# Two layers of attention and MLP on one core: which score maxima are taken beside the projections, the pace there, and attention's written-out order

## The chip, the cores and the metric

The kernel runs on 1 core of one Trainium2 chip. The metric is the device time of one execution in microseconds (us). The engines are PE (matmuls; its weight loads are listed as PEld), DVE, ACT, POOL, and SP, which only issues DMAs here.

## The reference, cut to what matters

x has 2048 rows of 640; there are 32 heads of 20. The same two blocks run twice, with the same weights. All is fp32.

```
def _A_ref(x, wqkv, wo):
    qkv = (x @ wqkv).reshape(B, S, 3, H, Dh).transpose(2, 0, 3, 1, 4)
    q, k, v = qkv[0], qkv[1], qkv[2]
    scores = einsum("bhqd,bhkd->bhqk", q, k) * (Dh ** -0.5)
    p = softmax(scores, axis=-1)
    o = einsum("bhqk,bhkd->bhqd", p, v)
    return o.transpose(0, 2, 1, 3).reshape(B, S, D) @ wo
def _B_ref(x, w1, b1, w2, b2):
    h = x @ w1 + b1
    return (where(h > 0, h, 0) ** 2) @ w2 + b2

for _ in range(2):
    x = x + _A_ref(layernorm(x), wqkv, wo)
    x = x + _B_ref(layernorm(x), w1, b1, w2, b2)
```

The softmax is over 2048 keys, so each query of each head needs the maximum over its 2048 scores before its exponentials are taken.

## The kernel before, in words

**Precision and packing.** Operands are split into a high and a low part (F32R), and products are the sum of three partial ones. A head's scores take 60 partitions: query parts and key parts stacked. Two heads stand on partitions 0 to 59 and 64 to 123 of one tile, and their matmuls are issued one after the other on the two halves of PE. Four heads (two such pairs) are a group: eight groups, g = 0 to 7. Queries come in four blocks of 512 (qb), keys in four chunks of 512 (c). A block of attention is one (g, qb), numbered t = 4 g + qb, 32 in all; it has 16 key tiles of 128.

**A layer's stages.** `qkv` (projections, and maxima beside them), `attention`, then the output projection and the MLP. All engines' instructions stand in the order in which the Python code emits them; nothing is scheduled afterwards.

**Maxima.** They are computed by score matmuls with queries on the partitions (L654), in steps of (p, sub): p picks a pair of heads, sub a quarter of the query block; eight steps are a (g, qb, c). Two ways:
- *plain*: `smax` and `smax_two` reduce one chunk's scores on DVE (L665 in attention, L679 in `qkv`).
- *double*: two chunks at once. max(a, b) = a + relu(b - a). `d_kd` holds the difference of the keys of chunks 1 and 0 ("d") and 3 and 2 ("e"). `step_two` multiplies queries by the differences, and ACT takes the Relu (L687); `both_two` multiplies by the lower chunk's keys, and one DVE instruction (L694) adds both and keeps the maximum, followed by one that reads its accumulator. A double step is two matmuls of differences, two of keys, two Relus, two pairs of DVE instructions.

**Projections.** `qkv` goes through UNITS, numbered n: a unit is one of ten 128-row pieces (pos; ORDER maps it to keys or queries, and jj is the piece) for one of four blocks of 512 tokens (tb). The first FIRST = 4 pieces come token block by token block (n = 0 to 15), the others piece by piece. From n = 4 on each matmul is cut in two halves of 64 partitions, the second halves lagging 22 behind (`Halves`, L356 and L365). After each chain's first half a 1x1 DVE copy (`turned_t`, L358) reads its bank. After the 40 units come 16 v units of 320 columns (`v_unit`, tt), and then the lagging halves are caught up. `between(cost)` is called after each matmul; costs are 1 for q/k and 0.65 for v. When the sum of costs reaches the pace, `some()` emits one piece of maxima work: a plain pair (pace PLAIN_PACE) or one half of a double step, `step_two` or `both_two` (pace DOUBLE_PACE). STEPS says at which n a group of maxima or a list of DOUBLE joins the queue. What is left when all units are emitted is emitted in a loop after them, ahead of attention. These matmuls write PSUM banks 0 to 4 in turn (`ps_q`), the projections banks 5 to 7.

`proj_end` evicts a unit: it splits it into high and low parts on ACT and POOL. For key pieces 0 and 1 (`which and pos < FIRST`), it also keeps the even token block in `kf`, subtracts it from the odd one on POOL, splits the difference, and stores it to `d_kd`. `load_kd` loads differences (six DMAs), `load_k` keys (six DMAs), `load_q` queries. Piece jj holds rows 128 jj to 128 jj + 127; group g needs rows 80 g to 80 g + 79. `following` calls `tiles` for a group of maxima when it begins and for the next two after it. DOUBLE and the plain groups of before cover all maxima of groups 0, 1 and 2 (t = 0 to 11).

**Attention.** `attention` emits by the letters of a written-out order; ORDER_OF_BLOCK is repeated until all is done:
- a, b: scores of one head (L748) and its exponential (L758, 512 wide), for the first or second half of PE
- S: both heads at once, into two adjacent banks, with one exponential over 1024
- m, n: one maximum (`smax`, L654 and L665), first or second half
- V: values of one key tile for four heads (L763), which wait for that tile's exponentials, accumulated in bank 7

Banks 0 to 6 are given out by `Clock`, a table of expected times. The maxima of later blocks (`todo`) are taken ahead of their use; when `todo` is empty, m and n emit nothing. After a block, DVE copies the accumulator (L776) before the next block's first values may write it. `load_q` for a block and key loads for later groups are emitted in `begin`.

Of the kernel before, what the change touches and what calls it, by code (L numbers as in the profile page):

```python
# [9 lines left out]
F32R = mybir.dt.float32r  # L10
# [6 lines left out]
P = 128  # L17
# [7 lines left out]
QB = 512  # L25
NQB = S // QB
# [7 lines left out]
NBLK = NG * NQB  # L34
# [5 lines left out]
def tile_layers(  # L40
# [11 lines left out]
    nc = tc.nc  # L52
# [6 lines left out]
    dram = ctx.enter_context(tc.tile_pool(name="dram", bufs=1, space=DRAM))  # L59
# [3 lines left out]
    def name(p):  # L63
        n_alloc[0] += 1
        return f"{p}{n_alloc[0]}"

    def slot(shape, dtype, label):
        return arena.tile(shape, dtype, tag="slot", name=name(label))

    def dma(eng, dst, src):  # L70

        if dst.dtype == F32R:
            dst = dst.bitcast(F32)
        if src.dtype == F32R:
            src = src.bitcast(F32)
        eng.dma_start(dst, src)  # L76

    def xtile(label):
        return xpool.tile([P, D], F32, tag="x", name=name(label))
# [146 lines left out]
            sp.put(raw, k * 4, k * 4 + 2, 2, eng_hi, eng_lo)  # L226

    d_qk = dram.tile([2, 2, D, S], F32R, name="d_qk")
    d_kd = dram.tile([2, 2, 2 * P, QB], F32R, name="d_kd")
    d_v = dram.tile([S, H, 32], F32, name="d_v")  # L230
    d_o = dram.tile([D, NQB, 2 * QB], F32R, name="d_o")
    d_one = dram.tile([2, 2, QB], F32R, name="d_one")
# [21 lines left out]
    def split_to(dst_hi, dst_lo, src):  # L254

        nc.scalar.copy(dst_hi, src)
        nc.vector.tensor_sub(dst_lo, src, dst_hi.bitcast(F32))  # L257

    def split_on_pool(dst_hi, dst_lo, src, r=None, hi=None):

        if r is None:
            r = xtile("r")[:, :QB]
        nc.scalar.copy(r, src)
        (hi or pool_hi)(dst_hi, r)
        pool_lo(dst_lo, r, dst_hi.bitcast(F32))

    def pool_hi(dst, src):
        nc.gpsimd.tensor_copy(dst, src)  # L268

    def pool_lo(dst, a, b):  # L270
        nc.gpsimd.tensor_sub(dst, a, b)
# [68 lines left out]
    xt_, keys = {}, {}  # L340
# [42 lines left out]
    def proj_end(pos, tb, dst):  # L383
        ev = slot([P, 2, QB], F32R, "ev")
        which, jj = divmod(ORDER[pos], 5)
        rows = slice(jj * P, (jj + 1) * P)
        kd = None
        if which and pos < FIRST:


            if tb % 2 == 0 and jj == 0:
                keys["of"] = slot([P, 2, QB], F32, "kf")
            kf = keys["of"][:, jj, :]
            r = xtile("r")[:, :QB] if tb % 2 else kf
            split_on_pool(ev[:, 0, :], ev[:, 1, :], dst, r, nc.scalar.copy)
            if tb % 2:
                kd = slot([P, 2, QB], F32R, "kd")
                nc.gpsimd.tensor_sub(kf, r, kf)
                pool_hi(kd[:, 0, :], kf)
                pool_lo(kd[:, 1, :], kf, kd[:, 0, :].bitcast(F32))  # L400
                if jj:
                    del keys["of"]
        else:
            if tb or pos >= FIRST:
                split_on_pool(
                    ev[:, 0, :], ev[:, 1, :], dst, None, nc.scalar.copy if pos < FIRST else None
                )
            else:
                split_to(ev[:, 0, :], ev[:, 1, :], dst)

        def store():
            cols = slice(tb * QB, (tb + 1) * QB)
            dma(nc.sync, d_qk[which, :, rows, cols].rearrange("h p t -> p h t"), ev)
            if kd is not None:
                dma(nc.sync, d_kd[tb // 2, :, rows].rearrange("h p t -> p h t"), kd)

        return store
# [105 lines left out]
    k_t, q_t, v_t, mx_t, kept = {}, {}, {}, {}, {}  # L523
# [79 lines left out]
    def rows_of_heads(dst, src_of, segs, g):  # L603
        for par in range(2):
            for off, hl in segs:
                r0 = 64 * par + off
                src = src_of[hl, 4 * g * DH : (4 * g + 4) * DH]
                src = src.rearrange("(a b d) t -> b d a t", a=2, b=2)[par]
                dma(nc.sync, dst[r0 : r0 + DH], src)

    def load_k(g, c, keep):

        if not keep:
            k = slot([P, 2, QB], F32R, "k")
        elif (g % 4, c) in kept:
            k = kept[g % 4, c]
        else:
            k = kept[g % 4, c] = slot([P, 2, QB], F32R, "k")
            for par in range(2):
                dma(nc.sync, k[64 * par + 60 : 64 * par + 62], d_one)  # L620
        k_t[g, c] = k
        rows_of_heads(k, d_qk[1, :, :, c * QB : (c + 1) * QB], KSEG, g)

    def load_q(t):
        g, qb = divmod(t, NQB)
        q_t[t] = slot([P, 2, QB], F32R, "q")
        rows_of_heads(q_t[t], d_qk[0, :, :, qb * QB : (qb + 1) * QB], QSEG, g)
# [16 lines left out]
    def maxima(t):  # L644
        if t not in mx_t:
            mx_t[t] = small.tile([P, 4, 4, 4], F32, tag="mx", bufs=14, name=name("mx"))
            if t in PARTLY:
                nc.vector.memset(mx_t[t], LEAST)
# [182 lines left out]
    def prep_job():  # L831
# [15 lines left out]
    DOUBLE = [  # L847
        [],
# [5 lines left out]
    ]  # L854
    PARTLY = {g * NQB + qb for x in DOUBLE for g, qb, c in x}

    FIRST = 4
    PLAIN_PACE = 4.2  # L860
    DOUBLE_PACE = 1.97
    STEPS = {
        2: [("tiles", (0, 0, 0))],
        4: [("plain", (0, 0, 0)), ("tiles", (1, 0, 0))],
# [5 lines left out]
        12: [("double", 1)],  # L870
        15: [("double", 2)],
        19: [("double", 3)],
    }
    UNITS = [(tb, pos) for tb in range(NQB) for pos in range(FIRST)]
    UNITS += [(tb, pos) for pos in range(FIRST, 10) for tb in range(NQB)]

    def qkv(first, x_src, rest):

        pending, groups, work = [], [], []
        double, twos, begun = [], [], []  # L880
# [34 lines left out]
        def later(f, n):  # L915
            pending.append((state["n"] + n, f))
# [16 lines left out]
        def end_group(x):  # L933
            g, qb, c = x
            t = g * NQB + qb
            rest = [w[0] for w in work[:1] + twos[:1]] + [w[0][0] for w in begun[:1]] + groups + double
            if t == 0:
                left[t] -= 1 if c in range(4) else 2
                if left[t] == 0:
                    mrows_max(t)  # L940
                    store = mrows(t)
                    later_rows.append((state["n"] + 60, store))
                    later_rows.append((state["n"] + 75, lambda: mrows_load(t)))
            if (t or left[t]) and all(y[:2] != (g, qb) for y in rest[:4]):
                del q_t[t]
            use = {(y[0], y[2]) for y in rest + coming}
            use |= {(h, 2 * "de".index(y)) for h, y in use if y not in range(4)}
            for y in [y for y in k_t if y[0] == g and y not in use]:
                if g < 2 or y[1] not in range(4):
                    del k_t[y]  # L950
# [22 lines left out]
        def some():  # L973
# [4 lines left out]
            if begun and (len(begun) > 1 or not (double or twos)):  # L978
# [6 lines left out]
                if (p, sub) == PAIRS[-1]:  # L985
                    end_group(w[0])
                return DOUBLE_PACE
            if groups or work:
# [3 lines left out]
            if w:  # L992
                (g, qb, x), p, sub = w
                begun.append((w, step_two(g * NQB + qb, p, sub, x)))
            return DOUBLE_PACE

# [34 lines left out]
        for tt in range(NKT):  # L1031

            def end(store, tt=tt):
                later(store, 12)
                if tt % 4 == 3:
                    del xt_[tt // 4]

            v_unit(tt, run, end)
            if first:
                w_v.save_full(1)  # L1040
            if tt == 10:
                load_v(0, 0)
            if tt in (8, 9):
                for c in (0, 1) if tt == 8 else (2, 3):
                    assert (0, c) not in k_t
                    load_k(0, c, True)
            if tt == 11:
                load_k(3, 0, True)
                load_q(3 * NQB)
            if tt == 12:  # L1050
                for c in range(1, 4):
                    load_k(3, c, True)
            if tt == 13:
                load_q(1)
                load_q(3 * NQB + 1)
        while run.behind:
            run.catch()
        while double or twos or begun:
# [11 lines left out]


    ORDER_OF_BLOCK = (
        "bbannaVbamnabmVnabmnabVSnanbmVnambabmVSbmnaVSnabmVSnSmVbmamnSVbmanbanVan"
        "abmbmVbambannVbmabanmVSmbanVSnabmVSnSmVm"
    )

    def attention(first, x_src, first_rows):
        last = NBLK * NKT
# [3 lines left out]
        st_n, sm_n = [0, 0], [0, 0]  # L1082
        state = {"begun": -1, "done": 0, "acc": None, "debt": 0}
        clock = Clock()
        todo = [
            (t, p, sub, c)
            for t in range(NBLK)
            for c in range(4)
            for p, sub in PAIRS
            if (t, p, sub, c) not in done  # L1090
        ]
# [104 lines left out]
        for o in "abab":  # L1196
            op(o)
        while state["done"] < last:
            for o in ORDER_OF_BLOCK:
                op(o)  # L1200
        assert min(sm_n) == len(todo)
        q_t.clear()
# [227 lines left out]
```

## Time and profile before

| | us |
|---|---|
| median of 3 runs (3583.65 to 3587.55) | 3584.02 |
| the profiled execution, its own time | 3588.35 |
| its span | 3586.5 |
| layer 1, projections: start to the first values of attention | 343.87 |
| layer 1, attention: first to last values | 343.87 to 1387.2 |
| layer 2, first values of attention | 2124.62 |

| engine | busy us | share |
|---|---|---|
| PE | 3557.8 | 99% |
| DVE | 2650.9 | 74% |
| ACT | 2694.0 | 75% |
| POOL | 836.0 | 23% |

How to read what follows: a window's row has its limits and length, then for each engine the busy time and, in brackets, the number of instructions, then the granted share of the TensorE clock, the DMA engines' share and GB/s. With a filter only the filtered instructions are counted. A row of the order of time has start, duration, engine, line, operation, tiles written and read, and the count of merged instructions; in square brackets stands how long the engine was idle before and what ended the wait. A group's row has the count, the busy time and the mean duration in ns, then idle time before it. Matmuls are pipelined, so their durations overlap: the distance between starts is what a matmul costs.

### The profile page before, as it was taken

Reading aid. Unit: us, or ns where it says so; the run is one execution under the profiler, and the core shown is the slowest. Engines: PE = TensorE matmul, PEld = TensorE weight load, DVE = VectorE, ACT = ScalarE, POOL = GpSimd, SP = SyncE. Lnnn points to the kernel's source line nnn. Section 1 sums busy time; section 2 is a strip of 40 time slices with the busy share of each in tenths; the row PEclk is TensorE's granted clock in tenths of the full one; section 3 lists DMA queues with packets and bytes.
Section 4 is the critical chain, followed back from the end, with each engine's and each line's share of the span. In section 5 each row is a group of like instructions: output and inputs, shape, how many; then the busy total and the mean of one; then the engine's idle time right before and its main releaser. Section 6 shows DMA issues by size and latency. Waiting matters only on the chain.

```text
span 3586.5 us, 71057 instructions
## 1 busy us (share of the span) xinstructions
PE 3557.8 (99%) x25544; PEld 2151.0 (60%) x25544; DVE 2650.9 (74%) x5208; ACT 2694.0 (75%) x4742; POOL 836.0 (23%) x945
## 2 busy tenths in 40 slices
PE   8999999999999999999999999999999999999999
PEld 7998333333333336889989973333333333378998
DVE  8998888888888871445569988888888888625443
ACT  3888999999999994122238889999999999932221
POOL 5440334312121210122143201212112212101110
PEclk9999999999999999999999999999999999999999
DMA  7766454422212136622367552222222121365220
GB/s 242 231 223 198 138 170 147 141 78 71 60 49 60 54 102 218 234 74 74 103 193 226 191 174 67 79 73 63 67 83 56 42 60 51 111 234 209 75 81 37
DMA packets 282800, 433.85 MB, mean 121 GB/s; under 512 B 71188, under 2 KB 130324, under 8 KB 282448
## 3 DMA queue, kind: packets, MB, share of 16 engines
q1 hardware_dynamic: 281920, 427.61, 38.3%
q8 instruction: 202, 3.31, 0.4%
q10 hardware_dynamic: 528, 1.70, 0.2%
q14 instruction: 150, 1.23, 0.1%
HBM read 284.48 MB, written 144.68 MB: 120 GB/s over the span
## 4 chain that ended last, share of the span: by engine, by line
PE 94%; DMA 2%; DVE 1%; ACT 1%; SPq 0%; issue 0%; POOL 0%; ACTq 0%; DVEq 0%; POOLq 0%
PE banks L763 27%; PE banks L336 22%; PE banks L748 18%; PE banks L654 17%; PE banks L365 5%; PE banks L356 4%; ACT e L758 0%; SPq L76 0%; DMA k<-d_qk 0%; PE banks L461 0%; DMA ot<-d_o 0%; DVE r L1278 0%; DVE h L257 0%; ACT r L1277 0%; DVE mx L679 0%
## 5 line engine op out<-in xcount | busy, mean ns | idle before, releaser
L758 ACT ACTIVATE e<-banks 128x512 f32<-128x512 f32 (+1 forms) x3460 | 2040.8, 687 | 49.4 <-PE banks L748 11.5
L665 DVE TENSOR_REDUCE mx<-banks 128x1 f32<-128x512 f32 x2560 | 1620.7, 685 | 326.1 <-PE banks L654 294.4
L763 PE MATMUL banks<-e,vg 128*32 128x512 f32 x8192 | 1097.3, 605 | 6.1 <-ACT e L758 5.4
L654 PE MATMUL banks<-k,q 60*128 60x512 f32 x3392 | 1080.6, 411 | 6.3 <-DMA q<-d_qk 1.8
L748 PE MATMUL banks<-q,k 62*128 62x512 f32 x4096 | 1045.5, 441 | 0.0
L748 PEld LDWEIGHTS banks<-q,k 62*128 62x128 f32 x4096 | 514.5, 185 | 741.8 <-ACT e L758 467.6
L654 PEld LDWEIGHTS banks<-k,q 60*128 60x128 f32 x3392 | 579.3, 185 | 208.0 <-ACT e L758 64.7
L694 DVE CUSTOM_DVE_ANT_0 rl<-banks,rl 128x512 f32<-128x512 f32 x704 | 456.7, 688 | 24.5 <-PE banks L654 6.2
L687 ACT ACTIVATE rl<-banks 128x512 f32<-128x512 f32 x704 | 381.0, 601 | 52.3 <-PE banks L654 41.8
L763 PEld LDWEIGHTS banks<-e,vg 128*32 128x32 f32 x8192 | 163.8, 108 | 362.3 <-issue 262.6
L336 PE MATMUL banks<-w,h 128*128 128x320 f32 x2304 | 348.9, 310 | 2.6 <-DVE h L257 2.5
L1277 ACT ACTIVATE r<-banks,b_t 128x512 f32<-128x512 f32 x96 | 66.1, 688 | 377.8 <-PE banks L336 224.7
L336 PEld LDWEIGHTS banks<-w,h 128*128 128x128 f32 x2304 | 339.2, 188 | 11.4 <-DVE h L257 6.4
L336 PE MATMUL banks<-xnT,w 128*128 128x512 f32 x1440 | 329.7, 389 | 0.0
L365 PE MATMUL banks<-xnT,wqk 64*128 64x512 f32 x1080 | 327.3, 393 | 1.6 <-DVE turned_t L358 1.6
L356 PE MATMUL banks<-xnT,wqk 64*128 64x512 f32 x1080 | 327.2, 394 | 0.0
L336 PEld LDWEIGHTS banks<-xnT,w 128*128 128x128 f32 x1440 | 269.5, 188 | 55.3
L807 POOL TENSOR_TENSOR few<-few,minus_t 128x16 f32<-128x16 f32 x62 | 179.8, 2900 | 225.6 <-DMA few<-d_s 225.6
L654 PE MATMUL banks<-kd,q 60*128 60x512 f32 x704 | 208.9, 398 | 0.2
L365 PEld LDWEIGHTS banks<-xnT,wqk 64*128 64x128 f32 x1080 | 201.2, 187 | 12.9 <-DVE turned_t L358 2.1
L268 POOL CAST mr<-nt 128x32 fp32r<-128x32 f32 x64 | 13.4, 210 | 824.6 <-DVE nt L720 794.6
L356 PEld LDWEIGHTS banks<-xnT,wqk 64*128 64x128 f32 x1080 | 198.8, 186 | 10.2 <-issue 1.7
(91 smaller groups left out, 2789.5 us busy)
## 6 DMA issues: line engine op xcount, KB each, us to landing
q<-d_qk SPq DMA_DIRECT2D x888, 80.0 KB
d_qk<-ev SPq DMA_DIRECT2D x80, 512.0 KB
k<-d_qk SPq DMA_DIRECT2D x456, 80.0 KB
x<-d_x SPq DMA_DIRECT2D x96, 320.0 KB
d_o<-ot SPq DMA_DIRECT2D x248, 80.0 KB
ot<-d_o SPq DMA_DIRECT2D x38, 512.0 KB
d_v<-v SPq DMA_DIRECT2D x32, 512.0 KB
vg<-d_v SPq DMA_DIRECT2D x32, 512.0 KB
```

Of the source, the lines that this page charges most:

```text
L336: nc.tensor.matmul(dst, a, b, start=(n == 0), stop=(n == last))
L356: nc.tensor.matmul(dst, a[:64], b[:64], start=start, stop=last)
L365: nc.tensor.matmul(dst, a, b, start=False, stop=last, skip_group_check=True)
L654: nc.tensor.matmul(dst, q_t[t][b : b + 60, p, sub * P : (sub + 1) * P], k_t[t // NQB, c][b : b + 60, p, :], start=True, stop=True,)
L665: nc.vector.tensor_reduce(maxima(t)[:, 2 * p + par, sub, c : c + 1], dst, axis=AX.X, op=ALU.max)
L687: nc.scalar.activation(r, dst, AF.Relu)
L694: nc.vector.tensor_tensor_reduce(out=r[par], in0=dst, in1=r[par], scale=1.0, scalar=LEAST, op0=ALU.add, op1=ALU.max, accum_out=maxima(t)[: ...
L748: nc.tensor.matmul(dst, k_t[t // NQB, kt // 4][b : b + 62, p, (kt % 4) * P : (kt % 4 + 1) * P], q_t[t][b : b + 62, p, :], start=True, stop ...
L758: nc.scalar.activation(dst, src, AF.Exp, scale=SCALE)
L763: nc.tensor.matmul(acc[32 * h : 32 * h + 32, :], v_t[t // NQB, kt // 8][:, kt % 8, 32 * h : 32 * h + 32], es[p][:, par, :], start=(kt == 0 ...
L807: nc.gpsimd.tensor_tensor(few, few, minus_t, op=ALU.pow)
L1277: nc.scalar.activation(r, dst, AF.Relu, bias=b1_t[:, f : f + 1])
```

## The change

- A fifth list in DOUBLE: both doubles of group 3, query block 0 (t = 12), 16 steps. It joins the queue at n = 26. Their maxima leave attention's `todo`.
- Differences are now also made for key piece 2 (`jj < 3`), whose high part is cast on POOL as before; `d_kd` has a third piece.
- DOUBLE_PACE goes from 1.97 to 1.84.
- The loads at the end of `qkv` skip keys of group 3 that are already there, and preload queries of t = 13 and 14 (NEXT) in place of 12 and 13.
- ORDER_OF_BLOCK is another string: 20 m and 20 n instead of 21 each, 9 S instead of 10, 23 a and 23 b instead of 22 each, 16 V as before.
- Once `todo` is empty, whole passes of LAST_ORDER (8 S and 4 V) take the place of ORDER_OF_BLOCK.

```
-    d_kd = dram.tile([2, 2, 2 * P, QB], F32R, name="d_kd")
+    d_kd = dram.tile([2, 2, 3 * P, QB], F32R, name="d_kd")
...
-        if which and pos < FIRST:
-            if tb % 2 == 0 and jj == 0:
+        if which and jj < 3:
+            if tb % 2 == 0 and jj != 1:
                 keys["of"] = slot([P, 2, QB], F32, "kf")
-            kf = keys["of"][:, jj, :]
+            kf = keys["of"][:, jj % 2, :]
             r = xtile("r")[:, :QB] if tb % 2 else kf
-            split_on_pool(ev[:, 0, :], ev[:, 1, :], dst, r, nc.scalar.copy)
+            split_on_pool(
+                ev[:, 0, :], ev[:, 1, :], dst, r, nc.scalar.copy if pos < FIRST else None
+            )
...
+        [(3, 0, "d"), (3, 0, "e")],
     ]
+    NEXT = [t for t in range(3 * NQB, NBLK) if (3, t - 3 * NQB, "e") not in DOUBLE[4]]
...
-    DOUBLE_PACE = 1.97
+    DOUBLE_PACE = 1.84
...
         19: [("double", 3)],
+        26: [("double", 4)],
...
-            if tt == 11:
-                load_k(3, 0, True)
-                load_q(3 * NQB)
-            if tt == 12:
-                for c in range(1, 4):
-                    load_k(3, c, True)
+            if tt in (11, 12):
+                for c in (0, 1) if tt == 11 else (2, 3):
+                    if (3, c) not in k_t:
+                        load_k(3, c, True)
+                if tt == 11:
+                    load_q(NEXT[0])
             if tt == 13:
                 load_q(1)
-                load_q(3 * NQB + 1)
+                load_q(NEXT[1])
...
     ORDER_OF_BLOCK = (
-        "bbannaVbamnabmVnabmnabVSnanbmVnambabmVSbmnaVSnabmVSnSmVbmamnSVbmanbanVan"
-        "abmbmVbambannVbmabanmVSmbanVSnabmVSnSmVm"
+        "SnabmVSanmbVSanmbVSSmnVnabbanmVnabanmbVbabmnnaVnaabmbmVbmmbanaVnambmbaVb"
+        "amnmbaVnanbabmVSmnabVSmnabVSnabmVSanmbV"
     )
+    LAST_ORDER = "SSSVSSVSSVSV"
...
-            for o in ORDER_OF_BLOCK:
+            for o in LAST_ORDER if min(sm_n) == len(todo) else ORDER_OF_BLOCK:
                 op(o)
```

## The prediction

> **What bounds the kernel now.** The page first, then windows over the stages, then single instructions in order of time.
>
> ```profile
> span 3586.5 us, 71057 instructions
> PE 94%; DMA 2%; DVE 1%; ACT 1%; SPq 0%; issue 0%; POOL 0%; ACTq 0%; DVEq 0%; POOLq 0%
> ```
>
> The chain that ended last is 94% PE. The change touches two stages of each layer: the projections with the maxima beside them, and attention. How close the other engines follow PE there decides.
>
> First the projections (window, length, busy time and count of an engine; the first two rows are of all engines, then those of L654 on PE, then of L694 on DVE).
>
> ```profile
> 160.00:190.00 30.00, 30.00 (x260) 27.59 (x258) 28.57 (x94) 26.42 (x51) 11.97 (x14) 1.00 0.70 223
> 280.00:310.00 30.00, 30.00 (x360) 29.99 (x358) 29.36 (x99) 26.50 (x54) 1.68 (x4) 1.00 0.69 203
> ...
> 160.00:190.00 30.00, 25.04 (x88) 14.85 (x87) 1.00 0.70 223
> 280.00:310.00 30.00, 24.42 (x89) 15.06 (x89) 1.00 0.69 203
> ...
> 160.00:190.00 30.00, 28.13 (x87) 1.00 0.70 223
> 280.00:310.00 30.00, 28.83 (x89) 1.00 0.69 203
> ```
>
> Matmuls go two by two, one on each half of the partitions; I call two such a row. In the q/k stretch 260 matmuls are 130 rows in 30 us: 0.231 us a row. In the v stretch 89 matmuls of L654 are 44.5 rows, 10.3 us; the other 271 are 135.5 rows of 320 columns in 19.7 us: 0.146 us each. L694 has two instructions for a head, four for a double, so doubles stand 30/(87/4) = 1.379 us apart in the first stretch, 30/(89/4) = 1.348 in the second. By the pace of 1.97, and two calls to a double, 3.94 units lie between doubles: 3.94 q/k rows and two rows of the double are 5.94 x 0.231 = 1.372 us; 3.94/0.65 = 6.06 v rows and two are 0.885 + 0.462 = 1.347. Both are what is seen: PE's rows set the pace, DVE is busy 95 and 98%.
>
> Now the end of the projections, and what DVE can do when it is behind (start, duration, then the instruction).
>
> ```profile
> 336.90 0.69 DVE L694 CUSTOM_DVE_ANT_0 rl<-banks,rl 128x512 f32<-128x512 f32 x1
> ...
> 337.51 0.69 DVE L694 CUSTOM_DVE_ANT_0 rl<-banks,rl 128x512 f32<-128x512 f32 x1
> ...
> 338.12 0.69 DVE L694 CUSTOM_DVE_ANT_0 rl<-banks,rl 128x512 f32<-128x512 f32 x1
> ...
> 338.73 0.14 DVE L358 COPY turned_t<-banks 1x1 f32<-1x1 f32 x1
> 342.94 1.29 DVE L665 TENSOR_REDUCE mx<-banks 128x1 f32<-128x512 f32 x2 [4.07 <-PE banks L654]
> ...
> 338.93 2.02 PE L365 MATMUL banks<-wv,xnT 64*128 64x320 f32 x12 [0.52 <-DVE turned_t L358]
> 340.65 0.50 PE L748 MATMUL banks<-q,k 62*128 62x512 f32 x1
> ...
> 341.23 1.18 PE L748 MATMUL banks<-q,k 62*128 62x512 f32 x5
> ...
> 343.87 0.64 PE L763 MATMUL banks<-e,vg 128*32 128x512 f32 x4
> ```
>
> Back to back a head takes DVE 0.611 us (336.90, 337.51, 338.12), a double 1.222. The last double ends with the last v unit; PE drains its lagging halves, attention's first score starts at 340.65, its first values (L763) at 343.87.
>
> Attention: the starts of the values of successive key tiles, one block of 16 tiles, and the last two blocks.
>
> ```profile
> 366.94 1.07 PE L763 MATMUL banks<-e,vg 128*32 128x512 f32 x8
> ...
> 369.08 1.07 PE L763 MATMUL banks<-e,vg 128*32 128x512 f32 x8
> ...
> 370.98 1.06 PE L763 MATMUL banks<-e,vg 128*32 128x512 f32 x8
> ...
> 374.78 1.06 PE L763 MATMUL banks<-e,vg 128*32 128x512 f32 x8
> ...
> 376.93 1.06 PE L763 MATMUL banks<-e,vg 128*32 128x512 f32 x8
> ...
> 375.92 0.69 DVE L776 COPY o<-banks 128x512 f32<-128x512 f32 x1
> ...
> 376.93:409.62 32.69, 32.69 (x237) 12.65 (x235) 27.52 (x46) 31.93 (x56) 10.73 (x13) 1.00 0.54 166
> 1325.54:1357.33 31.79, 31.14 (x212) 10.27 (x211) 14.17 (x24) 31.23 (x55) 6.50 (x6) 1.00 0.35 104
> 1357.33:1387.20 29.87, 27.47 (x185) 7.60 (x186) 0.00 (x0) 28.70 (x52) 6.07 (x4) 1.00 0.64 204
> ```
>
> A tile of four rows takes 369.08 - 366.94 = 2.14 us, one of three 370.98 - 369.08 = 1.90; the difference, 0.24, is one row again. The old order puts four rows before ten of its 16 values and three before six (counting the longer of the two halves): 10 x 2.14 + 6 x 1.90 = 32.80, measured 32.69. So PE's rows set this stage too, up to block 30, where the maxima run out and ACT takes over:
>
> ```profile
> L758 ACT ACTIVATE e<-banks 128x512 f32<-128x512 f32 x2824 | 1478.2, 608 | 32.3 <-PE banks L748 11.4 <-PE banks L654 1.0
> ...
> L758 ACT ACTIVATE e<-banks 128x1024 f32<-128x1024 f32 x636 | 643.0, 1036 | 17.2 <-PE banks L654 0.2 <-PE banks L748 0.2
> ...
> 1343.49 5.99 ACT L758 ACTIVATE e<-banks 128x512 f32<-128x512 f32 x12
> ```
>
> Twelve narrow exponentials end 5.99 - 0.60 = 5.39 us after the first has ended: 0.490 us each; a wide one takes 1036 - 608 = 428 ns more, 0.918. The old block has 44 narrow and 10 wide: 30.7 us, under PE's 32.7.
>
> **The change part by part**, per layer. Counts are from the built programs' instruction order.
>
> *Maxima moved.* Attention loses 32 pairs (4 chunks x 8 steps), 32 rows; the projections gain 16 doubles of two rows, also 32. PE's matmuls are as many as before, so only packing and place can move the time.
>
> *Blocks of 20 pairs.* The new order has four rows before eight values and three before eight. Over blocks 0 to 29 that turns 60 tiles: 60 x 0.24 = -14.4 us; by the block's own 32.69 against 32.80, I take -14.2. ACT must follow: a three-row tile with a wide exponential is 0.918 + 2 x 0.490 = 1.898 against 1.90, and eight such stand in a row across the block's edge. It just fits (block: 46 narrow and 9 wide, 30.8 against 32.3). The accumulator's copy at the edge ends at 375.92 + 0.69 = 376.61, 1.83 after its values began at 374.78; the next values, now 1.90 after, clear it by 0.07. I cost both at nothing; if that cover goes, ACT's nearest row is four narrow ones, 1.96: up to +0.06 x 240 = +14.4, taken up below as a rival.
>
> *Last tiles in an order of four.* Only block 31 uses it. Both last blocks are ACT's: 31.79 + 29.87 = 61.66, with ACT work of 2 x 30.7. Afterwards 30.8 + 32 x 0.918 = 60.2: -1.3, of which PE's lead in the first eight tiles of block 30 keeps back 0.2: -1.1 (bounds -1.3 and 0).
>
> *Denser doubles.* In the q/k stretch the program has 591 rows where it had 574: 17 x 0.231 = +3.9. In the v stretch 169 rows of doubles for 158: 11 x 0.231 = +2.5. The spacing becomes (3.68 + 2) x 0.231 = 1.312 and 5.66 x 0.146 + 0.462 = 1.288. DVE needs 1.222 and, one per 15 rows, a copy of 0.14: 1.256 and 1.275. That is 96 and 99% of PE's spacing, with five banks between them, so a late DVE stops PE soon. Bounds: nothing, or the old spacing staying, 104 x 0.067 + 84.5 x 0.060 = +12.0. Nearer to the first, since heads do follow each other at 0.611: I take +1.0.
>
> *The tail.* Four doubles are left when the last v unit is done, and stand before attention on PE: six rows. The first score writes bank 0, and the sixth of the eight DVE instructions of these doubles reads that bank. From the first row: 0.5 (a matmul's duration) + 5 x 0.611 + 0.69 = +4.2 where the score stood. Queued behind it: all scores, so ACT's first exponentials and the first values. Bounds: six rows alone, 1.4, and four doubles after a matmul, 0.5 + 4 x 1.222 = 5.4.
>
> *DMAs and POOL.*
>
> ```profile
> L398 POOL TENSOR_TENSOR kf<-r,kf 128x512 f32<-128x512 f32 x8 | 10.6, 1323 | 0.0
> L271 POOL TENSOR_TENSOR kd<-kf,kd 128x512 fp32r<-128x512 f32 x8 | 10.5, 1307 | 0.6
> ...
> L268 POOL CAST kd<-kf 128x512 fp32r<-128x512 f32 x8 | 4.9, 612 | 0.5
> ...
> 1816.81 4.68 DMA k<-d_qk
> ```
>
> 14 more DMAs a layer stand on SP (two stores of key differences, twelve loads of them), and group 3's keys 0 and 2 load earlier. POOL gets three more operations for each of two differences: 1.32 + 1.31 + 0.61 us, in a stretch where it is busy 11.97 of 30. Loads are issued two groups ahead, 16 doubles or 21 us. Hidden, nothing; without that cover a landing like the 4.68 us above, once a layer.
>
> *The clock.* PE's share is low at the stage's end, and in layer 2 the granted clock (third from the end of a window's row) fell there.
>
> ```profile
> 2117.18:2120.59 3.41, 2.88 (x21) 2.61 (x19) 1.68 (x7) 0.42 (x1) 0.00 (x0) 1.00 0.68 267
> 2120.59:2124.01 3.42, 3.42 (x16) 2.96 (x14) 0.00 (x0) 2.07 (x5) 0.00 (x0) 0.50 0.24 99
> 2124.01:2127.42 3.41, 3.41 (x15) 1.20 (x15) 1.63 (x4) 2.39 (x6) 0.47 (x2) 0.50 0.48 148
> ...
> 2118.91 2.19 PE L365 MATMUL banks<-wv,xnT 64*128 64x320 f32 x12 [0.53 <-DVE turned_t L358]
> ...
> 2158.77 1.06 PE L763 MATMUL banks<-e,vg 128*32 128x512 f32 x8
> ```
>
> From the drained halves to the end of block 0 layer 2 takes 2158.77 - 2118.91 = 39.86 us, layer 1 376.93 - 338.93 = 38.00: the half clock cost 1.9. With PE waiting for DVE in the tail, layer 1 will meet it too: +1.9 once (bounds 0 and 3.8).
>
> The Trainium skill, page "TensorE: Matmul & The Clock Gate", section "Part 1: The HAM clock gate", says that the clock halves after an idle window of some 3.4 us and returns after a busy one. The length agrees (two windows of 3.41 at 0.50), the condition does not: the window before held 21 matmuls and waited only 0.53 us. By that condition the tail, with a matmul every 0.6 us or so, would cost nothing here and the forecast would be 3577.
>
> **Sum.** A layer: -14.2 - 1.1 + 3.9 + 2.5 + 1.0 + 4.2 = -3.7; two layers -7.4; the clock +1.9: -5.5 us. Against the profiled execution's 3588.35 that is 3582.9; against the median of the runs, 4.3 lower, 3578.5.
>
> **Rivals.**
> *The tail is hidden.* DVE has caught up, and only the six rows are paid; no stalls, no half clock: 2 x (-14.2 - 1.1 + 3.9 + 2.5 + 1.4) = -15: 3569. For it: DVE sat 4.07 us idle at this place. Against: the bank of the first score.
> *Attention is ACT's.* The eight tiles in a row have 0.002 us to spare. At half of the 0.06 each, +7.2 a layer: -5.5 + 14.4 = +8.9: 3593. Against: three such tiles stand in a row already, at 1.90. This would also be the change not doing what its 20 pairs say.
> *Slower: doubles keep their spacing.* The place is the bank ring between PE and DVE: if a double's round trip and not PE's row count makes 1.379 and 1.348, a smaller pace buys nothing. +12.0 - 1.0 = +11 a layer: -5.5 + 22 = +16.5: 3600. It decides from 2.8 us of stalls a layer beyond the 1.0. Against: the rows account for the spacing to 0.01 us.
>
> **How the numbers follow.** Forecast 0.48 (3574 to 3586), tail hidden 0.26, ACT 0.15, spacing 0.11. The range 3567 to 3593 leaves out the last and the edges. This measurement can tell 0.2%, 7.2 us, from no change. Faster by more: the hidden tail and a fifth of the forecast, 0.35; slower by more: the spacing and half of ACT, 0.18; same 0.47.
>
> **What would show it.** Attention's blocks at 32.2 to 32.3 us with eight tiles at 1.90 (at 1.93 or more, ACT wins). Doubles 1.31 and 1.29 us apart. First values of layer 1 about 11 to 12 us later than 343.87. A half clock in both layers near there. DVE idle ahead of attention gone. I am wrong if blocks stay near 32.7, or doubles at 1.35.

## The result, and the profile after

The changed kernel takes 3596.07 us (median of 8 runs, 3594.09 to 3600.69), the one before 3584.28 in the same comparison (8 runs, 3583.65 to 3587.55): ratio 1.0033, interval 1.0022 to 1.0044. It is slower by 0.33%, more than the 0.2% that this measurement can tell, and lies above the predicted range.

The profiled executions stand 3597.91 to 3588.35, +9.6 us; the medians differ by 11.8, since the profiled execution of the kernel before lies above all eight of its runs. By stages, in us, from starts of instructions in the trace (blocks 30 and 31 to the end of the last values):

| | before, layer 1 / 2 | after, layer 1 / 2 | predicted difference, a layer |
|---|---|---|---|
| first to last projection matmul | 326.4 / 315.6 | 341.6 / 325.3 | +7.4 |
| last projection matmul to first values | 2.8 / 3.2 | 8.6 / 8.1 | +4.2, clock +1.9 once |
| attention, first to last values | 1042.2 / 1043.6 | 1030.3 / 1029.9 | -15.3 |
| of it, block mean (1 to 29) | 32.71 / 32.73 | 32.35 / 32.32 | -0.47 |
| of it, blocks 30 and 31 | 61.61 / 61.54 | 59.56 / 59.54 | -1.1 |

Attention gives 12.0 and 13.7 us, the stages ahead of it take 21.0 and 14.6, the rest differs by -0.3. So the slowdown is in the projections and the tail behind them. Lines of the changed kernel stand two lower: L654, L694, L748, L763 of before are L656, L696, L750, L765. First windows over the projections, all engines:

```profile
130.00:160.00 30.00, 30.00 (x254) 27.37 (x251) 28.95 (x99) 26.82 (x54) 16.37 (x18) 1.00 0.67 222
160.00:190.00 30.00, 30.00 (x257) 29.01 (x255) 29.05 (x96) 26.93 (x52) 11.98 (x14) 1.00 0.73 232
280.00:310.00 30.00, 30.00 (x352) 29.63 (x350) 29.52 (x100) 26.85 (x55) 1.67 (x4) 1.00 0.56 168
1955.00:1985.00 30.00, 30.00 (x255) 28.27 (x253) 29.07 (x97) 26.09 (x51) 11.86 (x14) 1.00 0.60 177
```

The same view for L696 on DVE alone:

```profile
160.00:190.00 30.00, 28.67 (x89) 1.00 0.73 232
280.00:310.00 30.00, 29.05 (x91) 1.00 0.56 168
```

PE issues 254 to 257 matmuls in 30 us of the q/k stretch where it issued 260, and never shows as idle: the ends of matmuls are modelled in this profile, so small delays do not appear, and the count is the measure. Over three windows of each stretch (91, 89, 89 and 93, 91, 93 instructions of L696) doubles stand 1.338 and 1.300 us apart; before it was 1.379 and 1.348, by rows it should be 1.312 and 1.288.

The tail, in order of time: DVE, then PE.

```profile
352.95 0.14 DVE L358 COPY turned_t<-banks 1x1 f32<-1x1 f32 x1
355.99 0.69 DVE L696 CUSTOM_DVE_ANT_0 rl<-banks,rl 128x512 f32<-128x512 f32 x1 [2.90 <-PE banks L365]
...
360.27 0.69 DVE L696 CUSTOM_DVE_ANT_0 rl<-banks,rl 128x512 f32<-128x512 f32 x1
...
352.39 3.09 PE L365 MATMUL banks<-wv,xnT 64*128 64x320 f32 x20
...
356.74 0.50 PE L656 MATMUL banks<-k,q 60*128 60x512 f32 x1 [0.35 <-DVE mx L696]
...
359.80 2.87 PE L750 MATMUL banks<-q,k 62*128 62x512 f32 x7 [0.72 <-DVE mx L696]
```

And the windows of the clock there:

```profile
356.80:360.20 3.40, 2.45 (x8) 0.97 (x8) 3.40 (x11) 1.66 (x4) 0.00 (x0) 1.00 1.02 407
360.20:363.60 3.40, 2.93 (x10) 1.59 (x9) 1.46 (x5) 2.81 (x5) 0.00 (x0) 0.50 0.23 93
363.60:367.05 3.45, 3.45 (x13) 1.16 (x15) 1.03 (x3) 1.54 (x4) 0.46 (x2) 0.50 0.90 200
```

DVE stands idle for 2.90 us while PE drains the lagging halves with no maxima between them; then eight heads follow at 0.611 us, the first score waits for the sixth of them, and the clock halves for 6.8 us, two windows.

Attention: the starts of the values around a block's edge and the copy that frees the accumulator:

```profile
460.49 1.07 PE L765 MATMUL banks<-e,vg 128*32 128x512 f32 x8
462.51 1.06 PE L765 MATMUL banks<-e,vg 128*32 128x512 f32 x8
...
461.68 0.69 DVE L778 COPY o<-banks 128x512 f32<-128x512 f32 x1
```

A window of a block's length, begun two tiles ahead of block 4 (494.81), and the last two blocks:

```profile
490.93:523.22 32.29, 32.28 (x238) 12.27 (x239) 26.42 (x44) 31.53 (x56) 15.50 (x19) 1.00 0.55 170
1335.94:1367.36 31.42, 30.57 (x209) 9.89 (x209) 11.28 (x19) 31.29 (x56) 6.49 (x6) 1.00 0.35 105
1367.36:1395.50 28.14, 27.15 (x184) 7.38 (x183) 0.00 (x0) 27.01 (x30) 6.07 (x4) 1.00 0.59 184
```

The mean over the blocks, tile by tile: 1.977 us at the edge (the tile from 460.49), 1.927 for the fourth, 1.90 for the other six with three rows, 2.12 to 2.14 for the eight with four.

One wait reaches PE in layer 1 that did not before. (In the kernel before, POOL too waits for stores of `ev`, 3.4 us at 146 us in layer 1 and twice in layer 2, but PE does not wait behind it.) The chain of work that ended last, between 205 and 245 us (start, duration, what):

```profile
213.42 4.60 DMA kd<-d_kd
218.04 4.18 DMA k<-d_qk
222.24 0.42 SPq L76
222.75 3.99 DMA d_qk<-ev
```

What SP issued in these microseconds (start, time from the first to the last of a row, count):

```profile
211.29 3.31 SPq L76 DMA_DIRECT2D kd<-d_kd  x6
214.93 3.38 SPq L76 DMA_DIRECT2D k<-d_qk  x6
218.45 3.28 SPq L76 DMA_DIRECT2D q<-d_qk  x6
...
222.75 0.72 SPq L76 DMA_DIRECT2D d_qk<-ev  x1
```

The waits from 222 to 232 us (who waited at which line for whom: total, times, longest):

```profile
POOL ev L268 <- DMA d_qk<-ev: 4.7, 1, 4.7
...
ACT r L263 <- POOL ev L271: 1.9, 1, 1.9
PE banks L656 <- ACT rl L689: 1.6, 1, 1.6
```

The window over this stretch:

```profile
195.00:240.00 45.00, 43.38 (x352) 38.83 (x350) 40.08 (x134) 38.59 (x75) 24.91 (x27) 0.96 0.71 235
```

SP issues one DMA after the other: eighteen loads of differences, keys and queries from 211.29 to 221.73 us, and the store of `ev` only at 222.75. POOL waits 4.7 us for the buffer that this store frees, ACT for POOL, with the Relus queued behind it, and PE 1.6 us for a Relu; one window of half clock follows, 3.4 us from 230.5 (0.96 in the mean over this row).

### The profile page after: what moved, and what is told of

It reads as the page before. It is cut to its first block, busy times and chain, and to the rows that moved or that the text cites. A ratio compares the mean times of both kernels' runs of the same rounds, so it can differ in the third digit from the quotient of the medians.

```text
span 3596.1 us, 71237 instructions
## 1 busy us (share of the span) xinstructions
PE 3564.3 (99%) x25544; PEld 2143.6 (60%) x25544; DVE 2611.4 (73%) x5210; ACT 2711.1 (75%) x4824; POOL 849.4 (24%) x957
## 4 chain that ended last, share of the span: by engine, by line
PE 92%; DMA 2%; ACT 2%; DVE 2%; issue 1%; POOL 1%; SPq 1%; POOLq 0%; ACTq 0%; DVEq 0%
PE banks L765 27%; PE banks L336 21%; PE banks L750 17%; PE banks L656 16%; PE banks L365 5%; PE banks L356 4%; ACT e L760 1%; DMA d_qk<-ev 1%; PE banks L351 1%; SPq L76 1%; DMA kd<-d_kd 1%; PE banks L463 0%; DVE mx L681 0%; DVE r L1284 0%; DVE h L257 0%
## 5 line engine op out<-in xcount | busy, mean ns | idle before, releaser
L667 DVE TENSOR_REDUCE mx<-banks 128x1 f32<-128x512 f32 x2432 | 1548.3, 685 | 369.5 <-PE banks L656 303.3
L765 PE MATMUL banks<-e,vg 128*32 128x512 f32 x8192 | 1094.8, 605 | 4.2 <-ACT e L760 3.0
L750 PE MATMUL banks<-q,k 62*128 62x512 f32 x4096 | 1042.1, 442 | 1.7 <-DVE mx L696 0.7
L656 PE MATMUL banks<-k,q 60*128 60x512 f32 x3328 | 974.1, 410 | 9.3 <-DVE mx L681 3.9
L750 PEld LDWEIGHTS banks<-q,k 62*128 62x128 f32 x4096 | 512.3, 185 | 649.0 <-ACT e L760 396.7
L656 PEld LDWEIGHTS banks<-k,q 60*128 60x128 f32 x3328 | 524.8, 186 | 310.5 <-ACT e L760 201.4
L696 DVE CUSTOM_DVE_ANT_0 rl<-banks,rl 128x512 f32<-128x512 f32 x768 | 492.1, 687 | 28.8 <-PE banks L365 8.1
L689 ACT ACTIVATE rl<-banks 128x512 f32<-128x512 f32 x768 | 415.5, 603 | 52.7 <-PE banks L656 40.9
L765 PEld LDWEIGHTS banks<-e,vg 128*32 128x32 f32 x8192 | 163.7, 108 | 363.1 <-ACT e L760 195.4
L356 PE MATMUL banks<-xnT,wqk 64*128 64x512 f32 x1080 | 337.5, 400 | 0.6 <-ACT r L263 0.6
L365 PE MATMUL banks<-xnT,wqk 64*128 64x512 f32 x1080 | 335.4, 396 | 0.0
L656 PE MATMUL banks<-kd,q 60*128 60x512 f32 x768 | 222.7, 408 | 2.6 <-ACT rl L689 2.4
L356 PEld LDWEIGHTS banks<-xnT,wqk 64*128 64x128 f32 x1080 | 200.3, 190 | 11.8 <-issue 1.7
```

What stands on the lines that cost most here:

```text
L356: nc.tensor.matmul(dst, a[:64], b[:64], start=start, stop=last)
L365: nc.tensor.matmul(dst, a, b, start=False, stop=last, skip_group_check=True)
L656: nc.tensor.matmul(dst, q_t[t][b : b + 60, p, sub * P : (sub + 1) * P], k_t[t // NQB, c][b : b + 60, p, :], start=True, stop=True,)
L667: nc.vector.tensor_reduce(maxima(t)[:, 2 * p + par, sub, c : c + 1], dst, axis=AX.X, op=ALU.max)
L689: nc.scalar.activation(r, dst, AF.Relu)
L696: nc.vector.tensor_tensor_reduce(out=r[par], in0=dst, in1=r[par], scale=1.0, scalar=LEAST, op0=ALU.add, op1=ALU.max, accum_out=maxima(t)[: ...
```

## The experiments

Stage times are those of the table above; layer 1 / layer 2. Where nothing else is said, an edit is to the changed kernel, and ratios are to the kernel before, run beside it on the same chip. Differences from the changed kernel are between comparisons; the medians of the kernel before in these are 3584.28 to 3586.06, so such differences hold to about 2 us.

**The tail: leftover doubles among the lagging halves.**

```
         while run.behind:
             run.catch()
+            if len(run.behind) % 3 == 0 and (double or twos or begun):
+                some()
```

> The four left doubles are emitted among the 22 lagging halves instead of behind them. Theory (in the changed kernel DVE sits idle 2.90 us while PE drains the halves, and then the first score waits for DVE's sixth instruction of the left doubles): the doubles start about 3 us earlier, the first values of attention come 3 to 4 us earlier in each layer, and the half clock after the tail costs less: 3586 to 3590 against 3596. Rival (the tail is PE and DVE work that has to be done somewhere, its order is no matter): the halves end later by what the doubles end earlier, 3594 to 3598.

3587.65 us, ratio 1.0007 [0.9998, 1.0017], 8.4 under the changed kernel. Projections and tail together are 3.5 / 3.0 shorter. The half clock behind the tail is gone in layer 2 (block 0 takes 32.3 us for 34.1) and 3.4 us long instead of 6.8 in layer 1. DVE and PE of this kernel, at the same place:

```profile
353.36 0.67 DVE L696 CUSTOM_DVE_ANT_0 rl<-banks,rl 128x512 f32<-128x512 f32 x1
...
357.77 0.69 DVE L696 CUSTOM_DVE_ANT_0 rl<-banks,rl 128x512 f32<-128x512 f32 x1
...
355.26 0.60 PE L365 MATMUL banks<-wv,xnT 64*128 64x320 f32 x3
357.30 0.50 PE L750 MATMUL banks<-q,k 62*128 62x512 f32 x1
```

The eight heads run from 353.36 on, while the halves drain, and the first score stands at 357.30. Most of the tail's price was the order of emission: of the 5.8 / 4.9 that it had grown by, 2.3 / 1.9 stay with the doubles.

**The buffer: one more slot.** The tiles of the projections come out of an arena of NSLOT slots; the room comes from two small pools.

```
-NSLOT = 42
+NSLOT = 43
-            mx_t[t] = small.tile([P, 4, 4, 4], F32, tag="mx", bufs=14, ...)
+            mx_t[t] = small.tile([P, 4, 4, 4], F32, tag="mx", bufs=13, ...)
-        mr = small.tile([P, 2, 32], F32R, tag="mr", bufs=2, ...)
+        mr = small.tile([P, 2, 32], F32R, tag="mr", bufs=1, ...)
```

> 43 buffers of 4 KB instead of 42 (one buffer of maxima and one of their transposed rows less). Theory (layer 1's stall at 228 us is POOL waiting for a buffer whose store is still queued on SP behind loads of differences; ACT stands behind POOL, Relus behind ACT, PE behind the Relus): the stall and the half clock after it go, layer 1's projections are 3 to 4.5 us shorter, layer 2's within 1 us: 3592 to 3593 against 3596. Rival (SP's queue or the loads themselves are late, and the wait only moves to another instruction): 3595 to 3597, with a PE gap over 1 us elsewhere in layer 1's projections.

3592.09 us, 1.0021 [1.0012, 1.0031], 4.0 under the changed kernel. Its row of the same stretch:

```profile
195.00:240.00 45.00, 45.00 (x384) 40.98 (x381) 42.13 (x141) 40.90 (x80) 25.49 (x27) 1.00 0.72 244
```

32 matmuls more in 45 us, none of which waits visibly, and full clock. The projections are 5.0 / 1.1 shorter. Of the 5.0, 1.6 come ahead of the 1050th projection matmul, before the wait; the buffer is worth the other 3.4. The stretch from the 1050th to the 1140th projection matmul of layer 1 shows it in every kernel: it takes 19.1 us in the changed kernel and 17.9 to 20.1 in the five others below with the dense pace and 42 buffers, 15.7 to 15.8 in the four with 43, and 14.9 to 15.1 in the four with the old pace.

**Both together.**

> Both repairs in one: left doubles among the lagging halves, and 43 buffers. Theory (two separate causes, the tail and layer 1's buffer): they add, 8.4 + 4.0 less than the changed kernel: 3583 to 3585, what the kernel before takes. Rival (both gains were one and the same half clock in layer 1): 3587 to 3588.

3583.51 us, 0.9994 [0.9985, 1.0003]: 12.6 under the changed kernel, the sum of the two within those 2 us. What is left equals the kernel before within the interval.

**The pace alone, in the kernel before** (`DOUBLE_PACE = 1.97` to `1.84`, nothing else).

> The kernel before with DOUBLE_PACE 1.84 alone: the same 22 groups of doubles, done some 45 units earlier. Theory (at the dense spacing DVE is the limit of the stretch, 1.30 to 1.34 us a double where PE's rows would give 1.29 to 1.31): rows that DVE delays are not won back by rows alone at the end, 1 to 3 us a layer: 3586 to 3590; spacing 1.30 in the v stretch. Rival (the dense pace costs nothing by itself, the projections' growth comes from the sixteen further doubles and their differences alone): 3584 within 1.5.

3594.22 us, 1.0025 [1.0016, 1.0034]: +8.6, more than either forecast allowed. The same number of rows takes 332.1 / 317.5 us where it took 326.4 / 315.6, +5.7 / +1.9. 3.1 of the 5.7 lie in the stretch of the late buffer, which the forecast did not have; the rest, 2.6 / 1.9, is within the 1 to 3 us a layer of its theory. Two windows:

```profile
160.00:190.00 30.00, 30.00 (x257) 28.99 (x256) 29.10 (x97) 26.78 (x53) 13.16 (x14) 1.00 0.73 234
1955.00:1985.00 30.00, 30.00 (x254) 28.26 (x253) 29.07 (x97) 26.49 (x52) 11.41 (x14) 1.00 0.54 167
```

And its waits from 205 to 240 us:

```profile
POOL ev L268 <- DMA d_qk<-ev: 5.2, 1, 5.2
...
PE banks L654 <- ACT rl L687: 2.1, 1, 2.1
```

The counts are those of the changed kernel, and the same buffer is late, without the new loads and differences. The denser pace brings both.

**The old pace, in the changed kernel** (`1.84` to `1.97`): (104 + 84.5) x 0.13/1.84 = 13 doubles a layer go from the projections to the tail.

> The changed kernel with the old DOUBLE_PACE of 1.97: some 13 doubles more a layer are left behind the v units. Theory (a double costs two rows, 0.46 us, beside the projections and 1.22 us of DVE in the tail): 13 x 0.76 = +9.9 a layer, less about 2.5 of stalls that the dense pace brings: +7 a layer, 3610. Rival (the dense pace stalls PE as much as it fits in, so that the pace is worth nothing): 3596 within 3 us.

3605.85 us, 1.0059 [1.0044, 1.0074], between the two forecasts. The projections are 16.1 / 13.2 shorter, the tail 18.2 / 18.3 longer. Layer 1's 16.1 holds the 3.4 of the late buffer, which the old pace does not meet. A double beside the projections thus costs (16.1 - 3.4)/13 and 13.2/13, some 1.0 us, where its two rows are 0.46; standing alone, 1.4. A window in the tail of this kernel:

```profile
330.00:360.00 30.00, 29.08 (x159) 20.74 (x156) 25.65 (x83) 22.69 (x44) 0.00 (x0) 0.74 0.66 204
```

**Is DVE the limit at the dense pace?** The 1x1 copy on ACT, on top of both mendings:

```
-                nc.vector.tensor_copy(turned_t, dst[:1, :1])
+                nc.scalar.copy(turned_t, dst[:1, :1])
```

> The kernel with both repairs, and the 1x1 copy after each chain's first half on ACT instead of DVE (some 68 a layer). Theory (at the dense pace DVE, 97 to 98% busy, holds PE's rows back: 254 matmuls in 30 us where there were 260): DVE is freed of 8 to 9 us a layer, the rows return to 258 or more, the projections are 3 to 5 us a layer shorter, 3574 to 3578 against 3583.5. Rival (it is the round trip through the five banks, ACT's part of it as much as DVE's): rows stay at 254 to 255, 3582 to 3587.

3583.23 us, 0.9994 [0.9985, 1.0003], as without it.

```profile
130.00:160.00 30.00, 30.00 (x254) 27.21 (x252) 28.60 (x91) 27.20 (x59) 16.10 (x17) 1.00 0.69 230
160.00:190.00 30.00, 30.00 (x256) 28.68 (x255) 28.71 (x92) 27.16 (x58) 12.70 (x14) 1.00 0.71 229
```

With both mendings alone the same two windows have 28.83 and 29.11 us of DVE, 26.89 and 26.76 of ACT, and 254 and 257 matmuls. So DVE is freer, ACT fuller, and PE's count does not rise: the forecast that freeing DVE gives the rows back failed. A late DVE is not the one limit. The traces say as much: of the about 220 matmuls of maxima that PE starts between 130 and 205 us, some start within 0.15 us of the last release that they needed: 7 released by DVE and 10 by ACT in the kernel before, 23 and 22 in the changed kernel, 21 and 26 with both mendings, and 22 and 24 with the copy on ACT besides.

**And what if DVE has more?** The copy twice, in the changed kernel and in the kernel before.

> The changed kernel with that copy twice on DVE: 68 x 0.14 = 9.5 us of DVE more a layer. Theory (DVE is the limit at 1.84): most of it is paid, 5 to 8 us a layer, 3606 to 3612. Rival (PE's rows or the banks are the limit, DVE has room): under 2 us a layer, 3596 to 3600.

> The kernel before with that copy twice on DVE: the same load at the pace of 1.97. Theory (DVE at 95% has 5% left, which the copies nearly fill): a smaller part is paid than in the changed kernel, 1 to 4 us a layer, 3587 to 3593. Rival (each copy delays PE by its own length wherever it stands, whatever the pace): the same rise as in the changed kernel.

3603.66 us, 1.0048 [1.0033, 1.0064], and 3589.65, 1.0009 [1.0000, 1.0019]: +7.6 on the changed kernel, between its two forecasts, and +3.8 on the one before, as its theory has it. The projections take 343.9 / 328.5 and 329.3 / 314.4: +2.3 / +3.2 at the dense pace, +2.9 / -1.2 at the old one, of which +1.1 / +0.8 come behind the 480th projection matmul. The tails do not grow (7.9 / 8.1 and 2.8 / 3.1). One v window of the changed kernel with two copies:

```profile
280.00:310.00 30.00, 30.00 (x344) 29.57 (x343) 29.51 (x107) 26.52 (x53) 1.68 (x4) 1.00 0.52 161
```

344 matmuls where it had 352. In the q/k stretch it issues 251 to 255; the kernel before with two copies issues 259 and 260 there, and 354 where it had 360 in this v window. So more work on DVE costs PE rate in the v stretch at both paces, and in the q/k stretch only at the dense one. Less work on it gains nothing in either: with the copy on ACT the v windows from 250 and from 280 us hold 354 and 349 matmuls, 354 and 350 without that.

**The old order of blocks, in the changed kernel** (LAST_ORDER kept).

> The changed kernel with the old order of blocks; LAST_ORDER takes over from block 29, since 608 pairs at 21 a block end in block 28. Theory (the two parts are independent: projections 35 us longer over both layers, attention's blocks 32.72 instead of 32.34, the last three blocks at 29.4, 29.4 and 28.1): attention 5 to 6 us a layer longer than in the changed kernel, 3605 to 3610; the projections as in the changed kernel within 2 us a layer. Rival (the new order's start is what makes the tail long): the tail ahead of attention falls from 8.6 to under 6 us and the time stays under 3603.

3604.15 us, 1.0051 [1.0038, 1.0065]; attention 1036.8 / 1036.6, +6.5 and +6.7. The new order is worth that, given that 32 pairs have left. The whole kernel rises by less, 8.1, because its projections came out 1.6 / 1.5 and its tail 0.7 / 0.7 us shorter; the tail, 7.8 / 7.4, stays above the rival's 6.

**LAST_ORDER alone, in the kernel before.**

> The kernel before with LAST_ORDER alone. Theory (block 31 is ACT's, and wide exponentials take it from 29.8 to 28.1 us, as in the changed kernel): 1.7 a layer, 3581 against 3584. Rival (what follows attention waits for the DMAs of the last heads, and the gain is waited away there): 3584.

3582.82 us, 0.9991 [0.9983, 1.0000]. Blocks 30 and 31 take 32.06 and 28.14: 1.4 less a layer.

**The edge of the block elsewhere.** First the same cyclic order begun at its ninth tile, so that a tile of four rows stands at the edge ("bmmbanaVnambmbaV..." to "...VnaabmbmV").

> The same 16 tiles of the order, begun at the ninth, so that a four-row tile instead of a three-row tile follows a block's edge. Theory (at the edge the values wait for DVE's copy of the accumulator, which takes the three-row tile there from 1.90 to 1.98 us): the block goes from 32.33 to 32.25 us, 2.4 us a layer, 3591 against 3596. Rival (the 0.08 is ACT's, late after a run of three-row tiles): the block stays at 32.3, 3595 to 3597.

3599.31 us, 1.0039 [1.0024, 1.0054]. The edge tile takes 2.132, without delay, and the old edge tile 1.900; but the first tile of three rows behind the run of four now takes 2.046, so that the block does not fall to 32.25 but rises to 32.39. DVE and PE there:

```profile
563.82 0.21 DVE L711 TENSOR_REDUCE nm<-mx 128x16 f32<-128x64 f32 x1
564.13 0.21 DVE L722 STREAM_TRANSPOSE nt<-nm 128x32 f32<-128x32 f32 x1
...
564.49 1.07 PE L765 MATMUL banks<-e,vg 128*32 128x512 f32 x8
566.53 1.05 PE L765 MATMUL banks<-e,vg 128*32 128x512 f32 x6
```

The reduction of the maxima and its transpose, which DVE does once a block, fall just ahead of that tile. Then, on top of both mendings, the order begun at its fifth tile ("nabbanmVnabanmbV..." to "...SanmbVSSmnV"): the edge and DVE's once-a-block work both lie in the run of four rows.

> The kernel with both repairs, and the order of blocks begun at its fifth tile: all eight four-row tiles first, then the eight of three rows. Theory (two pieces of DVE work stand at fixed tiles of a block, the accumulator's copy at the edge and the maxima's reduction and transpose at its fourth tile; each delays a three-row tile there, 0.08 and 0.03 us, as the rotated order at its ninth tile delayed the first three-row tile, right behind the reduction and transpose, by 0.15): four-row tiles hide both, the block goes from 32.34 to 32.24 us, 3 a layer, 3577 to 3579. Rival (a run of eight three-row tiles behind eight of four loses somewhere whatever stands there, ACT having no room in it): the block stays at 32.34 or above, 3583 to 3587.

3579.56 us (3577.51 to 3582.77), 0.9984 [0.9975, 0.9993]: under both kernels, by 6.5 us and 16.5 us (the latter between comparisons), and just above its theory. All tiles of three rows take 1.89 to 1.91. But the blocks fall only to 32.28 / 32.30, by 0.07 / 0.03 from 32.35 / 32.33 with both mendings and the old start: the four-row tile at the edge takes 2.17, where the others take 2.12 to 2.14, so the edge is not wholly hidden. Two blocks:

```profile
388.71:420.93 32.22, 32.22 (x234) 12.32 (x232) 25.94 (x44) 31.56 (x57) 10.47 (x12) 1.00 0.45 129
420.93:453.27 32.34, 32.34 (x234) 12.50 (x233) 25.96 (x44) 31.64 (x57) 13.52 (x14) 1.00 0.56 174
```

## Why the prediction was wrong

The sum missed by 15.1 us between the profiled executions (+9.6 for -5.5), and by 17.6 between the forecast of 3578.5 and the median. Of the signs that were named for being wrong, blocks near 32.7 did not come, and doubles at 1.35 only nearly (1.338 in the q/k stretch). By its own steps:

**"Denser doubles: I take +1.0" is the first step that failed**, with its rows taken at full rate. Projections were to grow by 7.4 a layer and grew by 15.2 / 9.7: 10.1 of the 15.1. The spacing came out 0.026 and 0.012 us over what rows give; over the prediction's 104 and 84.5 doubles that is 2.7 + 1.0 = 3.7 us of stalls a layer, not 1.0. So the term was 2.7 too small, 5.4 of the 10.1; 3.4 are the buffer below, and some 1.3 are left. The 3.7 lay inside my bounds, but I chose near the cheap end because heads do follow each other at 0.611 us. That shows DVE's rate with a full queue, and the argument named DVE as the one that would be late; the run with the copy on ACT does not bear this out. Matmuls that start right behind a release by DVE or ACT are two to three times as many as before (23 and 22 for 7 and 10), which points to the round trip of a double through five banks (PE, Relu on ACT, DVE, back to PE). ACT itself, which that run filled further, is not excluded, and whether a sixth bank would restore 260 matmuls was not tried: the cause of these stalls stays open.

**"DMAs and POOL: hidden, nothing" failed in layer 1.** The price that I named for lost cover, a landing of 4.68 us once a layer, was of the right size; the cover I named, loads issued two groups ahead, was not the one that mattered. A store behind loads was late, and with it a buffer. One slot gives back 4.0 us of the kernel's time, 3.4 of it in the stretch of the wait (shown). The new loads were not needed for it: the kernel before meets the same wait at the denser pace. Early in layer 1 there is also some half clock (10 us of it at 36 and 60 us, before 3.4 at 7.7) that comes and goes between kernels with the same start; I count it to neither.

**The tail was right, its clock in part by luck.** 4.2 a layer and the clock 1.9 once, 10.3 in all; measured with block 0, as the clock was reckoned, 5.8 + 4.9 + 0.6 = 11.3. The first score waits for the sixth of eight heads, as stated, and the half clock came in both layers. The long tail brings it every time: all six profiled kernels that have that tail, or a longer one, show it in both layers. But it also comes without: of the other eight, whose tails take 2.8 to 3.5 us, three show it there in layer 1 and three in layer 2. One of them, in both layers, is the kernel before with LAST_ORDER alone, whose projections and tail are those of the kernel before. So the +1.9 leans on the kernel before having been profiled without it in layer 1. "DVE idle ahead of attention gone" was wrong: 4.07 became 2.90 ahead of the eight heads and 1.74 behind them, since nothing is emitted among the draining halves. The Trainium skill, page "TensorE: Matmul & The Clock Gate", section "Part 1: The HAM clock gate", asks for an idle window; by that the tail would have cost no clock. The window ahead of the half clock holds 8 matmuls (356.80 above), so by that condition the trace disagrees. The same section's "A second HAM failure mode: psum-queue depth-cycling", which I had not weighed, says that frequent short idles between groups also make the clock swing; the trace agrees, with waits of 0.35 and 0.72 us in the tail.

**Attention was right in mechanism and short in size.** Blocks fell by 0.36 / 0.41, not 0.47. "The next values clear it by 0.07" failed: the copy ends at 461.68 + 0.69 = 462.37, 1.88 us after the values at 460.49, and the next stand at 462.51. The edge costs 0.08 a block and DVE's once-a-block work 0.03: 0.11 x 30 = 3.3 a layer. The two tiles of the order begun at its ninth tile show both; the last run recovers only a part of it. Against that, "last tiles: -1.1" measured -2.05. ACT, "just fits", did fit: three-row tiles with wide exponentials take 1.90, so that rival falls.

**The rivals.** "Doubles keep their spacing" gave 3600 and is nearest in time, but the spacing did shrink, by 0.041 of 0.067 and 0.048 of 0.060, and much of the time came from a buffer that it does not name. "The tail is hidden" did not happen; emitting the doubles among the halves makes most of it happen, and gives back 8.4.

## What to carry to other kernels

Work put beside a stretch that is already full can cost more than its rows: here a double more costs some 1.0 us for 0.46 of PE. Attention gave back 0.75 to 0.86 for it (12.0 and 13.7 a layer over 16; 1.4 a layer are LAST_ORDER's and need no move). With both mendings the move breaks even; with the order begun at its fifth tile besides, the kernel is 6.5 us faster than before, 2.8 of which LAST_ORDER alone brings. Try the denser pace alone first, and look where work that is left over is emitted: among instructions that drain anyway it costs little, behind them its whole chain. A fixed piece on a shared engine (a copy, a reduction) belongs in the tiles that have room, and a clearance of a few hundredths is none.

## What the hardware showed

- PE lost 1 to 2.3% of its matmuls per window (254 to 257 for 260) while it counted as 100% busy; only the count in a fixed window, or the distance of starts, showed it.
- The half clock lasted far longer than two windows where sparse matmuls went on: in the tail with the old pace 27.3 us of each layer, while PE issued two matmuls every 0.7 us or so (345.00 to 351.80 us: ten times two); the window above has 0.74 in the mean over 30 us with PE "busy" for 29.08.
